# Squared-ReLU attention and a routed expert layer on one core: straight query copies for the score matmuls

## The chip, the cores and the metric

The kernel runs on one core of a Trainium2 chip. TensorE multiplies matrices into PSUM, VectorE, ScalarE and GpSimd work elementwise, and SyncE only issues DMAs. The metric is the device time of one execution in microseconds. The profile calls the engines PE (PEld for TensorE's weight loads), DVE, ACT, POOL and SP.

## The reference

There are 8 sequences of 2496 tokens with 256 channels. Attention has no softmax: the scores are the product of z (64 wide) with itself. The expert layer routes each token whose skip score is positive to one of 8 experts.

```python
scores = (1 / S) * np.matmul(z, z.transpose(0, 2, 1))
attn = np.maximum(scores, 0.0) ** 2
x = (u * np.matmul(attn, v)).reshape(B * S, D)

do_compute = x @ w_skip > 0
xc = x[do_compute]
e_idx = np.argmax(xc @ w_gate, axis=1)     # gate_w: the softmax's largest value
for e in range(E):                          # 8 experts, 256 -> 1024 -> 256
    h = np.maximum(xc[mask] @ w1[e], 0.0)
    y[mask] = gate_w[mask, None] * (h @ w2[e])
out = x.copy(); out[do_compute] = xc + y
```

## The kernel before

**Chunks and steps.** The queries of a sequence (a batch, `b`) are taken in five chunks, `c` = 0 to 4: four of 512 and one of 448. This makes 40 chunks, `ci` = 5 b + c. For each chunk the keys are walked in ten steps `p` of 256 keys; `order` gives the order of the ten, and `k` is the place in it. In the numbers of the planner one chunk is `NB` = 20, so `at(s0 + 10, f)` runs `f` at the end of the chunk's step k = 5.

**Precision.** Each float32 operand is split into a high part that TensorE takes and the rest, `zh` and `zl`, `vh` and `vl`, `ah` and `al`; a product is three matmuls (high x high, high x low, low x high).

**A step.** `scores` (L242) multiplies the z of 256 keys (stationary) with the queries of the chunk (moving) into the PSUM tile `ps` (L251): three products for two groups of 128 keys, six matmuls, which are 64 deep and so run in pairs, one in each half of the array. ScalarE makes `r` from `ps` (ReLU L292, square L293). ScalarE or VectorE rounds `r` to `ah` (L315), and VectorE subtracts to get `al` (L319). `attend` (L346) multiplies v (stationary) with `ah` and `al` (moving) into the accumulators `acc`: 24 matmuls, 12 pairs, in a step, 18 in the one with p = 9. Step s makes the scores and weights of step s + 2 (`LA`), so TensorE has the scores of a later step between the attention matmuls of the current one.

**Recalled scores.** The score matrix of a batch is symmetric. For the pairs of chunks in `PAIRS` the weights are turned by VectorE (L268), written to `kept` and read back by SyncE (`recall`, L280) in place of computing them. Steps with recalled weights have no score matmuls.

**The order of tokens.** z and v are stored on the host with each 512 tokens in an order of their own (blocks of 32, the two block indices exchanged), so that recalled blocks fit. As keys, tokens are taken as they lie. As queries they must be in token order: `queries` (L235) reads a chunk of 512 with three nested loops, 16 runs of 32 columns. Chunks of 448 are read straight.

**End of a chunk.** `finish` multiplies by u and turns the result to rows `xrow`, which SyncE writes to `xr` and `out`. `routing` finds each token's expert and place for two chunks at a time; GpSimd writes the tokens to the experts' lists by indirect DMA (`put_in`, L505: two at the end of each of four steps, in the second half of one chunk and at k = 1 of the next). In the attention part this is GpSimd's only regular work.

**Experts.** After the 40 chunks `unit` handles 256 tokens at a time: GpSimd fetches their rows by indirect DMA (L556; VectorE first copies the indices, `go`, L554), TensorE turns them and does the two layers (L605, L624), VectorE adds to `o` (L653), and GpSimd scatters it to `out` (L654). Weights of the next expert are converted meanwhile, by GpSimd from expert 2 on (L151, L157).

**Buffers and order.** v and expert weights share `VBUFS` rotating tiles of 2 KB per partition: 20 per batch, two (`vh`, `vl`) for each of ten pairs of key blocks, and 16 per expert. `o` has two buffers of 2 KB and `o3` two of 1 KB in a pool of their own. Each engine executes its instructions in program order, which is written out by hand; between engines there are semaphores only. So GpSimd may run ahead of the step in whose code its instruction stands, as far as its operands and buffers allow.

Of the kernel before, what the change touches and what calls it, by code (L numbers as in the profile page):

```python
# [8 lines left out]
F32 = mybir.dt.float32  # L9
F32R = mybir.dt.float32r  # L10
# [7 lines left out]
P = 128  # L18
QC = 512
# [23 lines left out]
def f32(ap):  # L43
    return ap.bitcast(F32)
# [3 lines left out]
def attn_moe(ctx, tc, zT, uT, v, wg, w1, w2, cst, pad, out):  # L48
# [4 lines left out]
    nc = tc.nc  # L53
    B, _, SZ = zT.shape
    S = uT.shape[3]
    D = 2 * P
# [28 lines left out]

    zt, vt = {}, {}
    wts = {}
    VBUFS = 35

    def vtile(name):  # L90
        return vp.tile([P, 2, D], F32R, name=name, tag="v", bufs=VBUFS)
# [140 lines left out]
    kept = {x: dram.tile([QC, QC], F32, name="kept%d%d" % x) for x in PAIRS}  # L232
    HALF = (slice(0, 64), slice(64, 128))

    def queries(z, h, n):  # L235


        if n < QC:
            return z[h, :n]
        return z[h].rearrange("p (b a i) -> p a b i", b=4, a=4)  # L240

    def scores(b, q0, n, p):  # L242

        ps = ps_s.tile([P, 2, QC], F32, name="ps", tag="s")
        zh, zl = zt[b, p // 2]
        qh, ql = zt[b, q0 // QC]
        for m, (k, q) in enumerate(((zh, qh), (zh, ql), (zl, qh))):
            for x, h in enumerate(HALF):
                o = (2 * p + x) % 4 * P
                to = ps[:, x, :n] if n < QC else ps[:, x].rearrange("p (a b i) -> p a b i", b=4, a=4)  # L250
                nc.tensor.matmul(to, k[h, o : o + P], queries(q, h, n), start=(m == 0), stop=(m == 2))  # L251
        return ps

    def r_tile():
# [30 lines left out]
    def weights(ci, p, r=None, at_end=False):  # L285

        b, q0, n = chunks[ci]
        old, new = r, (ci % NQ, p // 2) in pairs(b)
        if not old:
            ps = scores(b, q0, n, p)  # L290
            r = r_tile()
            nc.scalar.activation(r[:, :, :n], ps[:, :, :n], AF.Relu, scale=isc)  # L292
            nc.scalar.activation(r[:, :, :n], r[:, :, :n], AF.Square)  # L293
        views, got = [], []

        def high():
            ah = ap.tile([P, 2, QC], F32R, name="ah", tag="ah")
            al = ap.tile([P, 2, QC], F32R, name="al", tag="al")
            got.extend((ah, al))
            if old and n < QC:  # L300

                b3 = 3 * P
                for x in range(2):
                    views.append(
                        [r.rearrange("p x (a k e) -> p x k a e", a=4, k=4)[:, x, :3]]
                        + [t[:, x, :b3].rearrange("p (k a e) -> p k a e", a=4, k=3) for t in (ah, al)]
                    )
                views.append(
                    [r.rearrange("p x (a k e) -> p x k a e", a=4, k=4)[:, :, 3, : (n - b3) // 32, :]]
                    + [t[:, :, b3:n].rearrange("p x (a e) -> p x a e", e=32) for t in (ah, al)]  # L310
                )
            else:
                views.append([x[:, :, :n] for x in (r, ah, al)])
            for r_, h_, _ in views:
                (nc.scalar.copy if on_act(ci, p) else nc.vector.tensor_copy)(h_, r_)  # L315

        def low():
            for r_, h_, l_ in views:
                nc.vector.tensor_sub(l_, r_, f32(h_))  # L319
            if new:  # L320
                if at_end:
                    put_off.append(lambda: keep(ci, p, r))
                else:
                    keep(ci, p, r)

        return got, high, low
# [252 lines left out]
    def unit(e, w, ids, xg, xt, fills=()):  # L579


        W = w * P
        xh, xl = xt
        w1h, w1l, w2t = wts[e]

        yb = [ps_acc.tile([P, 2, D], F32, name="y", tag="acc") for _ in range((w + 1) // 2)]
        ys = [yb[t // 2][:, t % 2, :] for t in range(w)]
        G = 2 if w < 3 else 1
        hs = []

        def h_part(p):
            ps = ps_h.tile([P, QC], F32, name="psh", tag="h")

            hh, hl = (
                ap.tile([P, 2 * QC], F32R, name="h" + c, tag=tag, bufs=k)[:, 80 : 80 + QC]
                for c, tag, k in (("h", "r", 5), ("l", "a" + "hl"[p % 2], 3))
            )
            for j in range(G):
                f = G * p + j
                m = 0  # L600
                for d in range(2):
                    k = 2 * d + f // 4
                    a, o = divmod((f % 4) * P, D)
                    for wt, x in ((w1h[k], xh), (w1h[k], xl), (w1l[k], xh)):
                        nc.tensor.matmul(  # L605
                            ps[:, j * W : (j + 1) * W], wt[:, a, o : o + P], x[:, d, :W],
                            start=(m == 0), stop=(m == 5),
                        )
                        m += 1
            nc.scalar.activation(hh[:, : G * W], ps[:, : G * W], AF.Relu)  # L610
            nc.vector.scalar_tensor_tensor(  # L611
                hl[:, : G * W], ps[:, : G * W], 0.0, f32(hh[:, : G * W]), op0=ALU.max, op1=ALU.subtract
            )
            hs.append((hh, hl))

        def y_part(p0, p1):

            fs = range(G * p0, G * p1)
            order = [(f, t) for t in range(w) for f in fs]
            for f, t in order:  # L620
                hh, hl = hs[f // G]
                tt = slice((f % G) * W + t * P, (f % G) * W + (t + 1) * P)
                for m, (h, k) in enumerate(((hh, 0), (hh, 1), (hl, 0))):
                    nc.tensor.matmul(  # L624
                        ys[t], h[:, tt], w2t[f][:, k, :],
                        start=(f == 0 and m == 0 and t % 2 == 0), stop=(f == NF - 1 and m == 2),
                        skip_group_check=True,
                    )

        np_ = NF // G  # L630
        last = np_ - 2
        parts = [(h_part, p) for p in range(3)]
        for p in range(3, np_):
            parts += [(h_part, p), (y_part, p - 3, p - 2)]
        if np_ == 4:
            parts += [(y_part, 1, 2)]
        else:
            last = np_ - 3
        parts += [(y_part, last, np_)]
        fills = dict(fills)  # L640
        for k, (f, *p) in enumerate(parts):
            f(*p)
            for g in fills.pop(k, ()):
                g()
        for k in sorted(fills):
            for g in fills[k]:
                g()
        o = op.tile([P, 2, D], F32, name="o", tag="o")
        for t in range(w):
            if t == 2:  # L650
                o = op.tile([P, 1, D], F32, name="o3", tag="o3")
            ot = o[:, t % 2, :]
            nc.vector.scalar_tensor_tensor(ot, ys[t], f32(ids[:, t, 1:2]), xg[t], op0=ALU.mult, op1=ALU.add)  # L653
            put = nc.gpsimd.indirect_dma_start(  # L654
                out=out,
                out_offset=bass.IndirectOffsetOnAxis(ap=ids[:, t, 0:1], axis=0),
                in_=ot,
                in_offset=None,
                bounds_check=N - 1,
                oob_is_err=False,  # L660
            )
            if t:
                tc.declare_no_dep(put.ins, put0.ins, reason="the rows of a unit's tokens are distinct")
            put0 = put
# [11 lines left out]
    def at(s, f):  # L676

        todo.setdefault(s // 2, []).append(f)
# [30 lines left out]
    for ci, (b, q0, n) in enumerate(chunks):  # L709
        s0 = ci * NB  # L710
        if ci + 1 < NC:
            at(s0 + 12, lambda ci=ci: load_u(ci + 1))
        if ci == 0:
            first = [(4 * j - 8, j % 2, 3, load_z, j) for j in range(2, NZ)]
            first += [(2 * g - 4, 1, 4, load_v, g) for g in range(2, NB // 2)]
            for s1, _, k, load, j in sorted(first, key=lambda x: x[:2]):
                eng = nc.vector
                if s1 - k < 0:
                    at(s1, load(0, j, eng))
                else:  # L720
                    later(s1 - k, k, load, 0, j, eng)
            at(14, lay_pads)
        if q0 == 0 and b + 1 < B:

            jobs = [(load_v, 0, 1, 3), (load_z, 0, 1, 6), (load_v, 1, 2, 3), (load_z, 1, 2, 5), (load_v, 2, 2, 7)]
            jobs += [(load_v, 3, 3, 3), (load_v, 4, 3, 4), (load_v, 5, 3, 6), (load_v, 6, 3, 7)]
            jobs += [(load_v, 7, 4, 2), (load_z, 2, 4, 3), (load_v, 8, 4, 4), (load_z, 3, 4, 5)]
            jobs += [(load_v, 9, 4, 6), (load_z, 4, 4, 7)]
            for load, j, c, k in jobs:
                later(s0 + c * NB + 2 * k - 7, 7, load, b + 1, j, nc.vector)  # L730
# [285 lines left out]
```

## Time and profile before

| | |
|---|---|
| median of 3 runs | 1785.65 us (1785.43 to 1788.15) |
| the profiled execution | 1782.95 us, of which the span from the first to the last instruction is 1781.2 us |
| attention part | to about 1276 us of the span |
| granted TensorE clock | 0.999 |
| busy | PE 1760.8 us, DVE 1185.5, ACT 1159.5, POOL 446.9 |

A busy share is an average over the attention and the expert part. In a line of instruction groups stand the code line, engine, operation, output<-inputs, shapes, the count, the busy time, the mean of one in ns, and the idle time of the engine before them with what ended it. In the chain of waits a piece is a stretch in which the chain stayed on one line of one engine.

### The profile page before, as it was taken

Reading aid. Unit: us, or ns where it says so; the run is one execution under the profiler, and the core shown is the slowest. Engines: PE = TensorE matmul, PEld = TensorE weight load, DVE = VectorE, ACT = ScalarE, POOL = GpSimd, SP = SyncE. Lnnn points to the kernel's source line nnn. Section 1 sums busy time; section 2 is a strip of 40 time slices with the busy share of each in tenths; the row PEclk is TensorE's granted clock in tenths of the full one; section 3 lists DMA queues with packets and bytes.
Section 4 is the critical chain, followed back from the end, with each engine's and each line's share of the span. In section 5 each row is a group of like instructions: output and inputs, shape, how many; then the busy total and the mean of one; then the engine's idle time right before and its main releaser. Section 6 shows DMA issues by size and latency. Waiting matters only on the chain.

```text
span 1781.2 us, 40579 instructions
## 1 busy us (share of the span) xinstructions
PE 1760.8 (99%) x15844; PEld 1555.9 (87%) x15844; DVE 1185.5 (67%) x2113; ACT 1159.5 (65%) x1499; POOL 446.9 (25%) x421
## 2 busy tenths in 40 slices
PE   8999999999999999999999999999999999999997
PEld 6879878987887898788889888888999999999997
DVE  6877877787887787788778778777753433343332
ACT  8878877877788777778777877877633333333321
POOL 0102201211220120121112022012255556635621
PEclk9999999999999999999999999999999999999999
DMA  5476689478857947894794789488652323313210
GB/s 190 125 181 151 158 211 223 98 200 220 177 140 193 230 104 195 213 211 109 199 219 117 189 206 222 112 191 196 158 120 76 91 84 110 95 52 90 87 38 26
DMA packets 403763, 267.44 MB, mean 150 GB/s; under 512 B 205859, under 2 KB 334117, under 8 KB 403440
## 3 DMA queue, kind: packets, MB, share of 16 engines
q1 hardware_dynamic: 389440, 240.47, 55.2%
q0 software_dynamic: 13712, 22.99, 4.6%
q8 instruction: 141, 2.31, 0.6%
q14 instruction: 182, 1.49, 0.3%
q10 hardware_dynamic: 288, 0.17, 0.0%
HBM read 145.80 MB, written 118.39 MB: 148 GB/s over the span
## 4 chain that ended last, share of the span: by engine, by line
PE 86%; DMA 4%; ACT 3%; DVE 3%; issue 2%; SPq 1%; POOL 0%; DVEq 0%; POOLq 0%; ACTq 0%
PE acc L346 52%; PE psh L605 11%; PE y L624 11%; PE ps L251 10%; DMA out<-o,idt 2%; DVE al L319 2%; DMA r<-kept 1%; ACT ah L315 1%; PE psm L414 1%; SPq L280 1%; ACT r L292 1%; ACT r L293 1%; PE pst L574 1%; DVE rt L268 0%; DMA xr<-xrow 0%
## 5 line engine op out<-in xcount | busy, mean ns | idle before, releaser
L346 PE MATMUL acc<-ah,vh 64*128 64x512 f32 (+1 forms) x3120 | 661.6, 385 | 1.3 <-DVE ah L315 1.1
L346 PE MATMUL acc<-ah,vl 64*128 64x512 f32 (+1 forms) x3120 | 644.0, 383 | 0.0
L319 DVE TENSOR_TENSOR al<-r,ah 128x1024 fp32r<-128x1024 f32 (+3 forms) x464 | 479.1, 1048 | 190.9 <-ACT ah L315 181.1
L346 PE MATMUL acc<-al,vh 64*128 64x512 f32 (+1 forms) x3120 | 514.1, 385 | 1.5 <-DVE al L319 0.9
L505 POOL DMA_INDIRECT lst<-pair,dest x160 | 198.0, 1238 | 1052.1 <-DVE dest L503 952.4
L346 PEld LDWEIGHTS acc<-ah,vh 64*128 64x128 f32 x3120 | 347.2, 184 | 56.5 <-ACT ah L315 2.8
L292 ACT ACTIVATE r<-ps 128x1024 f32<-128x1024 f32 (+1 forms) x278 | 280.1, 1007 | 178.9 <-PE ps L251 170.0
L346 PEld LDWEIGHTS acc<-ah,vl 64*128 64x128 f32 x3120 | 346.0, 184 | 50.3 <-DVE vl L120 0.2
L346 PEld LDWEIGHTS acc<-al,vh 64*128 64x128 f32 x3120 | 320.8, 184 | 59.0 <-DVE al L319 10.9
L315 ACT CAST ah<-r 128x1024 fp32r<-128x1024 f32 (+3 forms) x381 | 330.4, 892 | 51.2 <-PE acc L346 38.3
L293 ACT ACTIVATE r<-r 128x1024 f32<-128x1024 f32 (+1 forms) x278 | 289.9, 1043 | 8.8
L610 ACT ACTIVATE hh<-psh 128x512 fp32r<-128x512 f32 (+1 forms) x172 | 98.8, 583 | 286.8 <-PE psh L605 246.6
L605 PE MATMUL psh<-xt,w1h 128*128 128x256 f32 (+1 forms) x1280 | 235.1, 285 | 2.3 <-issue 1.8
L624 PE MATMUL y<-w2t,hh 128*128 128x256 f32 x1328 | 235.9, 281 | 0.0
L611 DVE SCALAR_TENSOR_TENSOR hl<-psh,hh 128x512 fp32r<-128x512 f32 (+1 forms) x172 | 113.0, 670 | 137.2 <-ACT hh L610 129.3
L624 PEld LDWEIGHTS y<-w2t,hh 128*128 128x128 f32 x1328 | 202.3, 189 | 0.6 <-issue 0.6
L605 PEld LDWEIGHTS psh<-xt,w1h 128*128 128x128 f32 x1280 | 197.4, 189 | 3.2 <-issue 3.2
L624 PE MATMUL y<-w2t,hl 128*128 128x256 f32 x664 | 184.7, 278 | 1.3 <-DVE hl L611 1.3
L605 PE MATMUL psh<-xt,w1l 128*128 128x256 f32 (+1 forms) x640 | 181.9, 284 | 0.0
L268 DVE STREAM_TRANSPOSE rt<-r 128x512 f32<-128x512 f32 x244 | 158.3, 686 | 1.6 <-DMA kept<-rt 1.5
L251 PE MATMUL ps<-zh 64*128 64x512 f32 (+1 forms) x556 | 126.0, 398 | 4.8 <-ACT zh L108 4.8
L624 PEld LDWEIGHTS y<-w2t,hl 128*128 128x128 f32 x664 | 124.7, 188 | 1.6 <-DVE hl L611 1.5
(170 smaller groups left out, 1610.3 us busy)
## 6 DMA issues: line engine op xcount, KB each, us to landing
kept<-rt SPq DMA_DIRECT2D x244, 256.0 KB
r<-kept SPq DMA_DIRECT2D x488, 128.0 KB
raw<-in_v SPq DMA_DIRECT2D x80, 256.0 KB
ut<-in_uT SPq DMA_DIRECT2D x32, 512.0 KB
xr<-xrow SPq DMA_DIRECT2D x128, 128.0 KB
out<-xrow SPq DMA_DIRECT2D x128, 128.0 KB
raw<-in_w SPq DMA_DIRECT2D x64, 256.0 KB
zf<-in_zT SPq DMA_DIRECT2D x40, 256.0 KB
```

Source lines behind the costliest of these rows:

```text
L251: nc.tensor.matmul(to, k[h, o : o + P], queries(q, h, n), start=(m == 0), stop=(m == 2))
L268: nc.vector.transpose(t[:, :, 32 * k : 32 * k + 32], r[:, x, :].rearrange("p (m i) -> p m i", i=32))
L292: nc.scalar.activation(r[:, :, :n], ps[:, :, :n], AF.Relu, scale=isc)
L293: nc.scalar.activation(r[:, :, :n], r[:, :, :n], AF.Square)
L315: (nc.scalar.copy if on_act(ci, p) else nc.vector.tensor_copy)(h_, r_)
L319: nc.vector.tensor_sub(l_, r_, f32(h_))
L346: nc.tensor.matmul(acc[t][:, :n], w[h, x, dd], a[h, x, :n], start=(first and t not in halves[:m]), stop=(last and t not in halves[m + 1 :]),)
L505: put = nc.gpsimd.indirect_dma_start(out=lst, out_offset=bass.IndirectOffsetOnAxis(ap=dest[:, t : t + 1], axis=0), in_=pair[:, t, :], in_o ...
L605: nc.tensor.matmul(ps[:, j * W : (j + 1) * W], wt[:, a, o : o + P], x[:, d, :W], start=(m == 0), stop=(m == 5),)
L610: nc.scalar.activation(hh[:, : G * W], ps[:, : G * W], AF.Relu)
L611: nc.vector.scalar_tensor_tensor(hl[:, : G * W], ps[:, : G * W], 0.0, f32(hh[:, : G * W]), op0=ALU.max, op1=ALU.subtract)
L624: nc.tensor.matmul(ys[t], h[:, tt], w2t[f][:, k, :], start=(f == 0 and m == 0 and t % 2 == 0), stop=(f == NF - 1 and m == 2), skip_group_c ...
```

## The change

For every chunk of 512 queries but the very first, GpSimd copies the z tiles of the queries (`zh` and `zl`) once into tiles `zq` in token order (`straight`); the copy stands in the code at the end of step k = 5 of the chunk before. The score matmuls of these chunks then read a flat row of 512 columns and write a flat row of PSUM. The copies need four tiles of 2 KB per partition. They come from `o` and `o3`, whose tiles now rotate in the same buffers, and from one tile less for v and weights.

```diff
-    VBUFS = 35
+    VBUFS = 34
...
-    def queries(z, h, n):
-        if n < QC:
-            return z[h, :n]
-        return z[h].rearrange("p (b a i) -> p a b i", b=4, a=4)
-
-    def scores(b, q0, n, p):
+    zq = {}
+
+    def straight(ci):
+        b, c = ci // NQ, ci % NQ
+        zq[ci] = [zp.tile([P, QC], F32R, name="zq" + x, tag="zq" + x, bufs=2) for x in "hl"]
+        for t, z in zip(zq[ci], zt[b, c]):
+            nc.gpsimd.tensor_copy(
+                t.rearrange("p (a b i) -> p a b i", a=4, b=4),
+                f32(z).rearrange("p (b a i) -> p a b i", b=4, a=4),
+            )
+
+    def queries(ci, k, h, n):
+        if n < QC or ci in zq:
+            return (zq[ci] if ci in zq else zt[ci // NQ, ci % NQ])[k][h, :n]
+        return zt[ci // NQ, ci % NQ][k][h].rearrange("p (b a i) -> p a b i", b=4, a=4)
+
+    def scores(ci, p):
+        b, _, n = chunks[ci]
         ps = ps_s.tile([P, 2, QC], F32, name="ps", tag="s")
         zh, zl = zt[b, p // 2]
-        qh, ql = zt[b, q0 // QC]
-        for m, (k, q) in enumerate(((zh, qh), (zh, ql), (zl, qh))):
+        flat = n < QC or ci in zq
+        for m, (k, q) in enumerate(((zh, 0), (zh, 1), (zl, 0))):
             for x, h in enumerate(HALF):
                 o = (2 * p + x) % 4 * P
-                to = ps[:, x, :n] if n < QC else ps[:, x].rearrange("p (a b i) -> p a b i", b=4, a=4)
-                nc.tensor.matmul(to, k[h, o : o + P], queries(q, h, n), start=(m == 0), stop=(m == 2))
+                to = ps[:, x, :n] if flat else ps[:, x].rearrange("p (a b i) -> p a b i", b=4, a=4)
+                nc.tensor.matmul(to, k[h, o : o + P], queries(ci, q, h, n), start=(m == 0), stop=(m == 2))
...
-            ps = scores(b, q0, n, p)
+            ps = scores(ci, p)
...
-        o = op.tile([P, 2, D], F32, name="o", tag="o")
+        o = zp.tile([P, 2, D], F32, name="o", tag="zqh", bufs=2)
...
-                o = op.tile([P, 1, D], F32, name="o3", tag="o3")
+                o = zp.tile([P, 1, D], F32, name="o3", tag="zql", bufs=2)
...
+            if chunks[ci + 1][2] == QC:
+                at(s0 + 10, lambda ci=ci: straight(ci + 1))
```

## The prediction

> **What bounds the kernel now.** I read the page first: which engine is busy, at what clock, and who carries the chain that ended last.
>
> ```profile
> PE 1760.8 (99%) x15844; PEld 1555.9 (87%) x15844; DVE 1185.5 (67%) x2113; ACT 1159.5 (65%) x1499; POOL 446.9 (25%) x421
> ...
> PEclk9999999999999999999999999999999999999999
> ...
> PE 86%; DMA 4%; ACT 3%; DVE 3%; issue 2%; SPq 1%; POOL 0%; DVEq 0%; POOLq 0%; ACTq 0%
> ```
>
> TensorE is busy for 99% of the span, at full granted clock throughout, and holds 86% of the chain. So time is won by making its instructions shorter, and lost by anything that makes it wait. The question is therefore how long a score matmul with the broken-up queries takes beside one with a straight operand. Means of single matmuls don't tell this, because two matmuls run in the two halves of the array at once and overlap their neighbours. The chain of waits does: where it stays on TensorE, a piece's length is the pace of its matmuls. Its columns are start us, length us, and what.
>
> ```profile
> 375.15 0.70 PE ps L251 x6
> 375.85 2.76 PE acc L346 x24
> 378.61 0.70 PE ps L251 x6
> 379.31 2.76 PE acc L346 x24
> ...
> 392.60 0.70 PE ps L251 x6
> 393.30 6.16 PE acc L346 x54
> 399.46 0.70 PE ps L251 x6
> 400.16 6.84 PE acc L346 x60
> 407.00 0.70 PE ps L251 x6
> ```
>
> All of these are 512 columns wide. Read three things. First, six score matmuls, three pairs, take 0.70 us: 0.233 a pair. Second, the attention matmuls have two paces. The piece of 60 is longer than the piece of 24 by 36 matmuls, or 18 pairs, and by 6.84 - 2.76 = 4.08 us: 0.2267 a pair. The piece of 54 gives the same, (6.16 - 2.76) / 15 = 0.2267. But the first 12 pairs behind a score group take 2.76 us, 0.230 each. So TensorE needs some pairs after a score group to fall back into its even pace, and these cost 2.76 - 12 x 0.2267 = 0.04 us. Third, a whole step with scores takes 0.70 + 2.76 = 3.46 us, where 15 even pairs would take 3.40. A score group thus costs 0.02 us itself and 0.04 us behind itself.
>
> Is it the broken-up operand, or scores as such? The last chunk of a batch has 448 columns, and its queries are read straight already:
>
> ```profile
> 301.81 0.61 PE ps L251 x6
> 302.42 1.22 PE acc L346 x12
> 303.63 0.61 PE ps L251 x6
> 304.24 3.65 PE acc L346 x36
> ```
>
> Scores: 0.61 / 3 = 0.203 a pair. Attention right behind them: 1.22 / 6 = 0.203, and over 18 pairs 3.65 / 18 = 0.203. There is neither a dearer score pair nor a slow stretch behind it. So I put both down to the operand in 16 runs of 32 columns.
>
> **The change part by part.**
>
> *Straight queries.* How many groups change:
>
> ```profile
> L251 PE MATMUL ps<-zh 64*128 64x512 f32 x460 | 106.7, 405 | 4.8 <-ACT zh L108 4.8
> L251 PE MATMUL ps<-zl,zh 64*128 64x512 f32 x460 | 104.5, 395 | 0.0
> L251 PE MATMUL ps<-zh,zl 64*128 64x512 f32 x460 | 104.3, 394 | 0.0
> ```
>
> 3 x 460 = 1380 matmuls are 230 groups of six. The first chunk of batch 0 has ten steps and no copy, so 220 groups change: 220 x (0.02 + 0.04) = 13.2 us of TensorE time. Bounds: nothing, if flat scores stay at 0.233 a pair, and 13.2 if they take the even pace and don't break it. I take 13.2, because attention matmuls switch weights, moving tile and output bank inside those long pieces without losing the pace, and a straight score matmul differs from them in nothing else.
>
> *How much of it reaches the end.* The attention part's chain (20 to 1276 us):
>
> ```profile
> by line: PE acc L346 72.0%; PE ps L251 13.9%; DVE al L319 2.0%; DMA r<-kept 1.9%; ACT ah L315 1.6%; SPq L280 1.5%; PE psm L414 1.5%; ACT r L292 1.3%; ACT r L293 1.3%; issue 0.8%; DVE rt L268 0.6%; DMA xr<-xrow 0.4%; DVE pre L462 0.2%; SPq L
> ```
>
> TensorE holds 72.0 + 13.9 + 1.5 = 87% of it. Elsewhere (weights al and ah just in time at the turn of a chunk, recalled scores) a faster TensorE only waits longer; late next there is al. So 0.87 x 13.2 = 11.5 us.
>
> *The copies.* Two per chunk for 31 chunks: 62 more GpSimd instructions of 128x512, one operand in, one out. No such row exists; the nearest are these.
>
> ```profile
> L151 POOL TENSOR_TENSOR w1l<-raw,w1h 128x512 fp32r<-128x512 f32 x24 | 30.9, 1298 | 0.5
> L187 POOL CAST tri<-cs 128x128 bf16<-128x128 f32 x1 | 0.3, 289 | 2.9 <-DMA cs<-in_cst 2.9
> L194 POOL MEMSET run_cnt<- 128x8 bf16 x1 | 0.1, 98 | 0.0
> ```
>
> From 98 ns at 8 columns and 289 at 128 come 1.6 ns a column and an estimate of 0.29 + 384 x 0.0016 = 0.9 us. The ends are 0.65 (half the two-operand one) and 1.3. So 1.8 us a chunk on an engine that is mostly idle. When they run is set by GpSimd's own queue, which in the attention part holds only the list writes:
>
> ```profile
> 327.23 1.16 POOL L505 DMA_INDIRECT lst<-pair,dest  x1 [2.00 <-DVE dest L503]
> ...
> 340.79 0.97 POOL L505 DMA_INDIRECT lst<-pair,dest  x1 [3.75 <-DVE dest L503]
> 342.07 1.83 POOL L505 DMA_INDIRECT lst<-pair,dest  x1 [0.30 <-issue]
> 390.98 1.71 POOL L505 DMA_INDIRECT lst<-pair,dest  x1 [47.08 <-DVE dest L503]
> ```
>
> A copy is queued after the writes of the second step of its chunk at the latest, or of the chunk before, and waits only for z tiles loaded long ago and for the scores of the straight chunk two before it. So it is done three steps to a chunk ahead of its first score matmul, and TensorE's new wait for it costs nothing; were that cover gone, it would cost up to 31 x 1.8 = 56 us. Behind the copies stand the next list writes, 47 us idle in front; 1.8 us there harms nobody. No DMA is added, and SyncE's queue keeps its order.
>
> *What the copies do to VectorE.* Here the trace shows a price, in the expert part:
>
> ```profile
> L554 DVE COPY go<-idt x45: 151/159/2031, 1308.1 to 1729.4; 128x2 int32<-128x2 int32 x45
> ```
>
> A two-column copy that takes 159 ns at the median took up to 2031 while GpSimd worked on weights: VectorE can be held for as long as GpSimd's elementwise work. Whether al (two inputs in SBUF) is held too, no row shows: no such VectorE instruction meets GpSimd elementwise work. What a held al costs depends on whether TensorE is waiting for it:
>
> ```profile
> L319 DVE TENSOR_TENSOR al<-r,ah x464: 276/1218/1284, 10.0 to 1279.3; 128x1024 fp32r<-128x1024 f32 x107, 128x384 fp32r<-128x384 f32 x24, 128x896 fp32r<-128x896 f32 x16, 128x128 fp32r<-128x128 f32 x8
> ...
>   PEld acc L346: 10.9, 24
> ...
>   PE acc L346: 0.9, 5
> ```
>
> TensorE waited for al at 29 of 400 steps (7%); elsewhere al is early. If a pair of copies meets two al, half of the time with GpSimd first, each held 0.9 us, the loss is 31 x 2 x 0.07 x 0.9 / 2 = 2.0 us. Bounds: 0 (never held) and 31 x 1.8 = 56 us (every hold reaches TensorE in full); I take 2.0, near the lower end, for the 7%.
>
> *One v buffer fewer.* 34 buffers are 17 pairs. Pair 7, 8 or 9 of the next batch now takes what pair 0, 1 or 2 of this one held. They are converted after steps 2, 4 and 6 of the batch's last chunk, and pairs 0, 1 and 2 are read last in steps 1, 1 and 2. The last weights of expert 0 take pair 0 of the last batch, five steps after its last read. So nothing waits; with the cover gone, ScalarE would wait for up to one step, 3.4 us, at each batch. *Result tiles in the copies' buffers:* the same two deep, and first written when scores are long over: nothing. *Straight score output:* the old view was already in order in memory: nothing.
>
> **Sum.** -11.5 + 2.0 = -9.5 us against this execution's 1782.95 us (span 1781.2): 1773.4. The runs' median, 1785.65, lies 2.7 above it, and I forecast that: 1776.1.
>
> **The rivals.** *Only the score pairs gain* (the stretch behind them stays slow, being due to the switch of work): 0.87 x 220 x 0.02 = 3.8 us less 2.0, 1783.8. For it: some slowness also follows other work. Against it: the 448-column pieces.
>
> *The runs of 32 cost nothing.* The 0.233 would then be the scores' own, the gain 0, and the time 1785.65 + 2.0 = 1787.7. Against it speaks 0.203 beside 0.203 above; for it, that 448 columns never show the even pace (0.2267 x 448 / 512 would be 0.198), so that the two widths may not compare. By the Trainium skill ("SBUF — State Buffer", section "Specifications (TRN2)") reads lose only where a 16-byte line gets fewer than two hits; a run of 32 words fills eight lines, so by that page this rival holds. The 0.70 us against 0.68 for three even pairs speaks against that page, unless the runs cost elsewhere than in the lines.
>
> *Slower: copies hold VectorE at the turn of a chunk.* If each chunk's copies hold an al that TensorE is waiting for by one copy, the price is 31 x 0.9 = 28 us, less 11.5: 1802. It decides from 11.5 / 31 = 0.37 us per chunk on. For it speaks the 2031 ns; against it the 7%, and that half of the copies start behind the second step's list writes, away from the turn. The Trainium skill ("SBUF — State Buffer", section "SBUF: two separate sides") says that VectorE and GpSimd share a port pair as an exclusive lock, which a VectorE instruction with two SBUF inputs needs as well; the row of go agrees for a plain copy, and no run here shows it for al.
>
> **How the numbers follow.** Both gains 0.52, 1773 to 1780; only score pairs 0.20, 1782 to 1786; nothing gained 0.15, 1785 to 1789; slower by holds 0.13, 1790 to 1803. From 1772 (13.2 gained, no loss) to 1788 some 0.85 are inside; the likeliest case alone has 1773 to 1780. A measurement of this kernel tells 0.2%, 3.6 us, from no change. Faster: 0.52 and a little of the second case, 0.54. Slower: 0.13. Same: 0.33.
>
> **What would show it.** In the chain, score groups of 0.68 us instead of 0.70 and 24 attention matmuls behind them in 2.72 instead of 2.76; if the second stays at 2.76, the first rival holds, if both stay, the second. A GpSimd group of 62 copies near 0.9 us. An al group whose longest is far over 1284 ns and a larger wait of TensorE for al would show the holds. The prediction is wrong if straight scores break the even pace too, or if the saved time comes back as waits for al.

## The result and the profile after

The changed kernel takes 1773.57 us (median of 4 runs, 1771.19 to 1776.28) beside 1786.9 us for the kernel before: a ratio of 0.9934, 95% interval 0.9922 to 0.9946, or 11.8 us less (9.6 to 13.9). This is the recorded ratio; the quotient of the two medians is 0.9925, or 13.3 us. Two more sets of runs gave 0.9932 (0.9918 to 0.9945) and 0.9944 (0.9930 to 0.9957). It is faster by more than the runs scatter, and lies inside the predicted 1772 to 1788; the forecast was 1776.1.

The group of al from the page of the kernel before, then TensorE's busy line and the group of al from the page of the changed kernel:

```profile
L319 DVE TENSOR_TENSOR al<-r,ah 128x1024 fp32r<-128x1024 f32 (+3 forms) x464 | 479.1, 1048 | 190.9 <-ACT ah L315 181.1
```

```profile
PE 1751.5 (99%) x15844; PEld 1571.7 (89%) x15844; DVE 1196.0 (67%) x2113; ACT 1159.2 (65%) x1499; POOL 491.4 (28%) x483
...
L331 DVE TENSOR_TENSOR al<-r,ah 128x1024 fp32r<-128x1024 f32 (+3 forms) x464 | 488.4, 1068 | 185.2 <-ACT ah L327 175.4
```

TensorE has the same 15844 matmuls in 9.3 us less busy time. VectorE has the same 2113 instructions and is busy for 10.5 us more: al rose from 479.1 to 488.4 us in total.

In that first profile the chain breaks off at the end of the kernel; in a second execution of the same kernel (label change_again below) it is whole. The same stretch as in the prediction:

```profile
377.48 0.68 PE ps L263 x6
378.16 2.72 PE acc L358 x24
380.88 0.68 PE ps L263 x6
...
391.27 0.68 PE ps L263 x6
391.95 6.12 PE acc L358 x54
398.07 0.68 PE ps L263 x6
398.75 6.80 PE acc L358 x60
```

A score group takes 0.68 us where it took 0.70, and the 24 attention matmuls behind it 2.72 where they took 2.76. Long pieces have shrunk by the same 0.04 only (6.80 from 6.84): it was their first pairs that were slow. 2.72 / 12 = 0.2267 us: straight scores keep the even pace, and a scored step takes 3.40 us in place of 3.46.

The copies, from line L242 of the same second execution (duration min/median/max in ns):

```profile
L242 POOL CAST zqh<-zh x31: 622/642/1413, 6.6 to 1177.2; 128x512 fp32r<-128x512 f32 x31
L242 POOL CAST zql<-zl x31: 605/626/1644, 7.7 to 1178.5; 128x512 fp32r<-128x512 f32 x31
```

### The profile page after: what moved, and what is told of

Read it like the earlier page. It is cut to its first block, busy times and chain, and to the rows that moved or that the text cites. A ratio compares the mean times of both kernels' runs of the same rounds, so it can differ in the third digit from the quotient of the medians.

```text
span 1772.5 us, 40706 instructions
## 1 busy us (share of the span) xinstructions
PE 1751.5 (99%) x15844; PEld 1571.7 (89%) x15844; DVE 1196.0 (67%) x2113; ACT 1159.2 (65%) x1499; POOL 491.4 (28%) x483
## 5 line engine op out<-in xcount | busy, mean ns | idle before, releaser
L358 PE MATMUL acc<-ah,vh 64*128 64x512 f32 (+1 forms) x3120 | 654.6, 383 | 1.2 <-DVE ah L327 0.6
L331 DVE TENSOR_TENSOR al<-r,ah 128x1024 fp32r<-128x1024 f32 (+3 forms) x464 | 488.4, 1068 | 185.2 <-ACT ah L327 175.4
L358 PE MATMUL acc<-al,vh 64*128 64x512 f32 (+1 forms) x3120 | 506.3, 383 | 2.2 <-DVE al L331 1.6
L666 POOL DMA_INDIRECT out<-o,idt x77 | 76.7, 996 | 171.4 <-DVE o L665 148.6
```

The source lines that it names most:

```text
L358: nc.tensor.matmul(acc[t][:, :n], w[h, x, dd], a[h, x, :n], start=(first and t not in halves[:m]), stop=(last and t not in halves[m + 1 :]),)
L666: put = nc.gpsimd.indirect_dma_start(out=out, out_offset=bass.IndirectOffsetOnAxis(ap=ids[:, t, 0:1], axis=0), in_=ot, in_offset=None, bou ...
```

## The experiments

**How they are compared.** Some kernels read the queries in another token order; then other tokens go to other experts, and the expert part has other work (15768 matmuls in place of 15844 with straight scores and no copies, 15694 and 15666 with runs of 8 and of 128). The first chunk also differs between executions of one kernel (34.0 to 34.5 us in the traces that have TensorE at full clock from 8 or 9 us of the span on, 35.5 to 36.5 where that comes at 13 to 14 us). So besides the ratios of whole runs I use a stretch that all have in common: in the chain, the long attention piece of batch 0's last chunk (x132) and that of the very last chunk (x96) each stand at the same place of the program in every kernel. From the start of one to the start of the other are 35 chunks: batches 1 to 7, with 10 + 8 + 6 + 4 = 28 scored steps of 512 columns each, 196 groups. In order: the changed kernel; the kernel before in a second execution; straight scores without copies; copies alone.

```profile
146.90 13.38 PE acc L358 x132
...
1255.45 10.12 PE acc L358 x96
```

```profile
147.71 13.38 PE acc L346 x132
...
1263.94 10.12 PE acc L346 x96
```

```profile
146.39 13.38 PE acc L346 x132
...
1254.84 10.12 PE acc L346 x96
```

```profile
147.31 13.38 PE acc L358 x132
...
1263.65 10.12 PE acc L358 x96
```

| label | median us | ratio to before, 95% | stretch us |
|---|---|---|---|
| before_again | 1783.18 | 1.0004 (0.9995 to 1.0013) | 1116.23 |
| change_again | 1771.2 | 0.9932 (0.9918 to 0.9945) | 1108.55 |
| change_third | 1772.31 | 0.9944 (0.9930 to 0.9957) | |
| flat_no_copies | 1768.27 | 0.9912 (0.9899 to 0.9926) | 1108.45 |
| copies_alone | 1783.33 | 0.9999 (0.9990 to 1.0008) | 1116.34 |
| buffers_alone | 1784.98 | 1.0002 (0.9993 to 1.0011) | |
| copies_on_scalar_engine | 1781.72 | 0.9989 (0.9980 to 0.9998) | 1114.36 |
| copies_three_times | 1794.98 | 1.0066 (1.0050 to 1.0081) | |
| one_product_in_runs | 1780.63 | 0.9984 (0.9975 to 0.9994) | 1114.07 |
| runs_of_8 | 1785.24 | 1.0009 (1.0000 to 1.0018) | 1127.46 |
| runs_of_128 | 1757.89 | 0.9856 (0.9841 to 0.9871) | |

Where the stretch is empty, the chain broke off, as in the first profile. The prediction's execution of the kernel before has 1262.64 - 146.30 = 1116.34: the stretch repeats within about 0.1 us. The change is worth 7.7 us in it.

**The mark: the changed kernel again (change_again).**

> The changed kernel, run again beside the three below. Every theory: 0.9934 of the kernel before, about 12 us less. It serves as the mark for the other runs of the same chip.

As expected.

**Straight scores without copies (flat_no_copies).**

```diff
-        return z[h].rearrange("p (b a i) -> p a b i", b=4, a=4)
+        return z[h]
...
-                to = ps[:, x, :n] if n < QC else ps[:, x].rearrange("p (a b i) -> p a b i", b=4, a=4)
+                to = ps[:, x, :n]
```

> The kernel before, but the score matmuls read the z tile of the queries as it lies in memory, one run of 512 columns. There are no copies, and buffers are as before. What is left out: the queries are not brought into token order, so the outputs belong to the wrong tokens; the number and size of all instructions are those of the kernel before. My theory (the runs of 32 columns cost TensorE 0.02 us per score group and 0.04 us behind it, and the copies cost a little): all 230 groups gain, 230 x 0.06 x 0.87 = 12 us, and the copies' price of about 2 us is not paid, so this is 1 to 3 us faster than the changed kernel, near 1773. Rival A (the copies cost nothing): the same time as the changed kernel within 1 us. Rival B (the gain of the change comes from something else, the new buffers or the copies' effect on other engines): no gain over the kernel before.

The whole run is 2.9 us shorter than the changed kernel's, which looks like the price of the copies that my theory foretold. It isn't: the stretch is 1108.45 against 1108.55, and the rest is the expert part with its 76 matmuls less (483.7 us from the last attention matmul to the last matmul, beside 487.3). So the straight operand alone gives the gain (rival B falls), and the copies cost nothing where they can be compared (rival A).

**Copies that nobody reads (copies_alone).** Only the test in `queries` and `flat` is taken back:

```diff
-        flat = n < QC or ci in zq
+        flat = n < QC
```

> The changed kernel with all its copies and buffers, but the score matmuls read the z tiles in 16 runs of 32 as before; nobody reads the copies. My theory: the gain is gone and the copies' holds of VectorE remain, 0.5 to 4 us slower than the kernel before (1787 to 1791); the longest al near 2400 ns as in the changed kernel, TensorE's wait for al up by 1 to 2 us. Rival A (the copies cost nothing): within 0.5 us of the kernel before. Rival B (the gain came from buffers or copies): about 12 us faster than before.

1116.34 in the stretch, 0.9999 in the runs: no gain and no loss. My 0.5 to 4 us of loss is refuted, although VectorE is held just as in the changed kernel, as the line of al shows (kernel before, second execution, then copies alone):

```profile
L319 DVE TENSOR_TENSOR al<-r,ah x464: 278/1218/1228, 10.0 to 1280.6; 128x1024 fp32r<-128x1024 f32 x107, 128x384 fp32r<-128x384 f32 x24, 128x896 fp32r<-128x896 f32 x16, 128x128 fp32r<-128x128 f32 x8
```

```profile
L331 DVE TENSOR_TENSOR al<-r,ah x464: 278/1220/2401, 9.8 to 1280.3; 128x1024 fp32r<-128x1024 f32 x107, 128x384 fp32r<-128x384 f32 x24, 128x896 fp32r<-128x896 f32 x16, 128x128 fp32r<-128x128 f32 x8
...
  PEld acc L358: 10.5, 23
...
  PE acc L358: 1.0, 5
```

The longest al doubles, and TensorE's wait for al (10.5 and 1.0 us) is what it was in the kernel before (10.5 and 1.0).

**What a hold looks like (changed kernel, timeline: start us, us, instruction).**

```profile
469.67 0.64 POOL L242 CAST zqh<-zh 128x512 fp32r<-128x512 f32 x1
470.00 2.39 DVE L331 TENSOR_TENSOR al<-r,ah 128x384 fp32r<-128x384 f32 x1
470.23 0.63 POOL L242 CAST zql<-zl 128x512 fp32r<-128x512 f32 x1
470.79 0.63 POOL L242 CAST zqh<-zh 128x512 fp32r<-128x512 f32 x1
```

Two chunks' copies stand together here, four in a row to about 471.97. The al that starts within the first takes 2.39 us where its like takes 0.54 (the mean of that shape in the kernel before), and gets its turn only when the last has ended. The same happens at four places of the execution, each in the last chunk of a batch, where al is early enough. It isn't so everywhere. At three other places an al gets in between the two copies of a pair:

```profile
596.65 1.70 DVE L331 TENSOR_TENSOR al<-r,ah 128x1024 fp32r<-128x1024 f32 x1 [2.73 <-ACT ah L327]
```

```profile
596.62 0.65 POOL L242 CAST zqh<-zh 128x512 fp32r<-128x512 f32 x1
597.18 1.64 POOL L242 CAST zql<-zl 128x512 fp32r<-128x512 f32 x1
```

This al ends 1.09 us after the first copy, and the second copy takes 1.64 us, to 598.82, in place of some 0.63. What decides whether VectorE gets in between two copies is not shown.

**Three times the copies (copies_three_times).**

```diff
-        for t, z in zip(zq[ci], zt[b, c]):
+        for t, z in 3 * list(zip(zq[ci], zt[b, c])):
```

> The changed kernel with each copy made three times, one after the other: 186 copies, up to 3.8 us of GpSimd in a row. Theory 1 (VectorE has room for being held, al is mostly early, which is why the 62 copies cost nothing): al grows by another 10 to 25 us in total, its longest to 3 us or more, but the chunks 1 to 39 of the attention part grow by less than 3 us over the changed kernel's 1230.8. Theory 2 (one pair of copies just fits, more doesn't): 5 us or more slower than the changed kernel. Beside that: TensorE's pause of about 2 us at the branch into the last expert, which the profiled kernels show except for the changed one; if it depends on where the code lies, it may come back here.

Theory 1 has failed: 1795 us against 1772, and al grew by 34.8 us where it allowed 10 to 25. The timeline at the same place, with twelve copies in a row, and TensorE's waits for al over the whole run:

```profile
476.31 0.65 POOL L242 CAST zqh<-zh 128x512 fp32r<-128x512 f32 x1
476.64 6.83 DVE L331 TENSOR_TENSOR al<-r,ah 128x384 fp32r<-128x384 f32 x1
```

```profile
  PEld acc L358: 26.9, 29
...
  PE acc L358: 15.6, 10
```

The al is held for 6.83 us, and here it is too late: TensorE waits 3.48 us for it, and right afterwards its granted clock is halved for 3.41 us (0.83 on average from 484 to 494 us; the score group at 486.35 takes 1.12 us). The wait and half of the 3.41 us, an estimate of what the clock costs, make 5.2 of the 5.3 us that such a chunk loses. The loss sits only where two chunks' copies meet, every second batch: these last chunks take 32.9 to 34.0 us where they take 27.6, four times some 5.3 us or more (6.4 in the first, where the clock is halved for 6.83 us), while six copies in a row (some 3.4 us) cost nothing: apart from the first, the other chunks are within 0.1 us of the changed kernel's. So theory 2 holds at four places, and theory 1 everywhere else. The changed kernel's four copies in a row still fit; there is no wide margin.

**Copies on ScalarE (copies_on_scalar_engine).**

```diff
-            nc.gpsimd.tensor_copy(
+            nc.scalar.copy(
```

> The changed kernel with the 62 copies on ScalarE in place of GpSimd. If the holds of VectorE by GpSimd are what keeps part of the gain back, the longest al falls back to about 1284 ns, and this is up to 2 us faster than the changed kernel, unless ScalarE's own 62 x 0.6 = 37 us, put in the order of its queue, make r and ah late. If the holds cost nothing, it is the same or slower: ScalarE is busy for 79% of the attention part, and two copies of 0.6 us in front of the next r cost up to 31 x 1.2 = 37 us where TensorE is waiting. I expect between 1 us faster and 4 us slower than the changed kernel.

The longest al is back at 1229 ns, and yet 1114.36 in the stretch: three quarters of the gain are lost (5.8 of 7.7 us), more than I allowed for; in whole runs it is 10.5 us slower than the changed kernel's 1771.2, where I expected 4 at most. TensorE's weight loads now wait for al 36 times:

```profile
  PEld acc L358: 15.8, 36
```

The holds were harmless; ScalarE's own work in their place is not. TensorE's waits for ah grew too, from 5.5 to 11.1 us (matmuls and weight loads together), so I read it as ah coming late and al behind it; no run tries this alone.

**Where the score pairs' time comes from: the number of runs (runs_of_128, runs_of_8).** Other factors in `queries`, no copies:

```diff
-        return z[h].rearrange("p (b a i) -> p a b i", b=4, a=4)
+        return z[h].rearrange("p (b a i) -> p a b i", b=2, a=2)   # or b=8, a=8
...    # and the same factors in the view `to` of the output in `scores`
```

> The kernel before, without copies, but the score matmuls of the chunks of 512 read the queries in 4 runs of 128 columns in place of 16 of 32. What is left out: the token order of the queries, so the outputs belong to the wrong tokens (and the routing in the expert part differs); all instructions are of the same number and size. Theory 1 (a broken-up operand costs TensorE per run: 6.5 ns a pair for 16 runs, so 0.4 ns per run): a score pair takes 0.2267 + 0.0016 = 0.228 us. Theory 2 (any pattern of more than one loop costs a fixed 6.5 ns): 0.233 as before. Behind the score group: whether an excess as small as that breaks the even pace of 0.2267 is open; if it does, the next nine pairs take 0.231 as before, if not, 0.227.

> The kernel before, without copies, but the queries are read in 64 runs of 8 columns. What is left out: the token order of the queries, as in the run with 4 runs. Theory 1 (a cost per run): 0.2267 + 64 x 0.0004 = 0.253 us a score pair, 3 x 0.020 us more per score group than before, so some 230 x 0.06 = 14 us slower than the kernel before, less what waits hide. Theory 2 (a fixed cost for the pattern): 0.233, the time of before. Theory 3 (only runs shorter than a line of SBUF cost, which 8 words of 4 bytes are not): 0.233 at most.

Four runs, timeline of TensorE (its chain broke off), and 64 runs, chain:

```profile
375.37 0.39 PE L251 MATMUL ps<-zh 64*128 64x512 f32 x2
375.60 0.39 PE L251 MATMUL ps<-zl,zh 64*128 64x512 f32 x2
375.82 0.39 PE L251 MATMUL ps<-zh,zl 64*128 64x512 f32 x2
...
378.77 0.39 PE L251 MATMUL ps<-zh 64*128 64x512 f32 x2
```

```profile
380.85 0.77 PE ps L251 x6
381.63 2.76 PE acc L346 x24
384.39 0.77 PE ps L251 x6
```

With four runs a scored step takes 378.77 - 375.37 = 3.40 us: nothing is left of the excess, of the pair or behind it. With 64 a pair takes 0.77 / 3 = 0.257 us (0.253 expected), and behind it stands the same 2.76 as with 16. So the cost goes by the number of runs, some 0.4 to 0.5 ns each, not by the pattern having several loops (theory 2), and a run of 8 words costs as well as one of 32 (theory 3). The 2 ns that four runs should cost by this don't show. With 16 and with 64 runs the pace is lost, with 4 it isn't. The kernel with 64 runs is 11.2 us longer in the stretch than the kernel before, where 196 groups at the expected 0.06 us make 11.8 (the 14 was for 230). That its runs come out at 1.0009 is due to the other routing, as is most of the 0.9856 with four runs: from the last attention matmul to the last matmul they take 479.4 and 472.0 us, the kernel before 489.4. In all these runs the output view changes together with the queries. It lies in order in memory every time, so I put the cost down to the queries; no run changes one without the other.

**The slow pairs behind a group (one_product_in_runs).** The first product in 16 runs, the other two straight:

```diff
+                flat = n < QC or m != 0
...    # where flat, the matmul reads q[h, :n] and writes ps[:, x, :n]
```

> The kernel before, without copies: of the three products of a score group only the first reads its queries in 16 runs of 32, the other two read one run of 512. What is left out: the token order of the queries in two products. Theory 1 (one slow pair is enough to break the even pace, which comes back some nine pairs later): the first pair takes 0.233, and the following pairs 0.230 on average over about ten, so a scored step keeps most of its excess, 3.44 to 3.46 us. Theory 2 (the excess behind the group grows with the number of slow pairs): a third of the excess, 3.42 us per scored step.

```profile
380.98 0.69 PE ps L252 x6
381.68 2.75 PE acc L347 x24
384.43 0.07 PE psm L482 x4
```

384.43 - 380.98 = 3.45 us, as theory 1 has it; a third of the excess would have been 3.42. One slow pair is enough: the pace is lost by being broken, not by how much. In the stretch only 2.2 of the 7.7 us are gained.

**Buffers alone (buffers_alone).** `VBUFS = 34`, and `o` and `o3` in the pool of the z tiles:

> The kernel before with the buffers of the changed kernel only: 34 tiles for v and weights, and the result tiles o and o3 in the pool of the z tiles; no copies, score matmuls as before. My theory: no wait is added, the kernel before within 0.1% (0.999 to 1.001). Rival (the places of the tiles matter in the expert part, which would explain why the attention part of the two profiled executions shrank by only 9 us and the runs by 12): 1 to 3 us faster than before, with a shorter expert part.

1.0002 (0.9993 to 1.0011): no effect, as the count of last reads said. The rival falls.

**Second and third executions (before_again, change_third).**

> The kernel before, unaltered, for a second profiled execution and as a mark of what a ratio near 1 is worth. Every theory: 0.999 to 1.001; chunks 1 to 39 of the attention part 1239.6 us as in the first; the first chunk anywhere from 34 to 36.5 us, since its loads differ from execution to execution; TensorE's pause of about 2 us at the branch into the last expert is there again if it belongs to this code.

> The changed kernel, unaltered, for a third profiled execution. Open is why the runs gained 12 us and the chunks 1 to 39 only 8.8. Theory 1 (the pause at the branch into the last expert is gone in the changed kernel, by where its code lies): no pause over 1 us at that branch here either, and the expert part 2 us shorter than in the kernel before. Theory 2 (the pause comes and goes by chance): it appears here, and the 3 us stay unexplained.

The kernel before against itself gives 1.0004, so the ratios can be trusted to about 0.1%. The pause at the branch into the last expert (some 450 us into the expert part) is there again, 1.5 us in the row of TensorE's waits that end in "issue" (the branch itself took part):

```profile
PE psh L605 <- issue: 1.5, 1, 1.5
```

With copies alone it is 2.2 us, and it is in the profiles of buffers alone, straight scores without copies, ScalarE's copies and one product too. It is in none of the three profiles of the changed kernel, nor with three times the copies. So it is hardly chance, but what it hangs on is not shown: no one part of the change takes it away. Nor is the expert part clearly 2 us shorter without it: from the last attention matmul to the last matmul the two executions of the kernel before take 489.4 and 487.7 us, the three of the changed kernel 490.0, 487.3 and 486.5.

## Why the prediction was right, point by point

**Two costs of the runs, in the score pairs and behind them: right, in size too.** 0.68 and 2.72 us stand where they were forecast. The first rival (only the score pairs gain) falls with 2.72; the second (the runs cost nothing), with the line rule of the Trainium skill ("SBUF — State Buffer", section "Specifications (TRN2)") beside it, falls with the runs of 8: those fill two 16-byte lines with four hits each, and cost the most. The row also gives a penalty for each cross to a new line, but 512 words lie in 128 lines in every one of these orders.

**How much reaches the end: the step that was too high.** I took 87%, TensorE's share of the chain. In the stretch it is 7.7 of 196 x 0.06 = 11.8 us, 65%. A share of the chain says where time lies, not what work stands behind each score group. Three things were left out. First, other work breaks the pace too. In the changed kernel, the gate matmuls (L426) and the list positions (L493):

```profile
370.13 1.00 PE psm L426 x26
371.13 2.94 PE acc L358 x24
...
384.28 0.07 PE psm L493 x4
384.35 0.78 PE ps L263 x6
385.13 2.75 PE acc L358 x24
```

And the gates in the kernel before, second execution:

```profile
372.68 1.00 PE psm L414 x26
373.68 2.94 PE acc L346 x24
```

And the list positions in its first execution, from the same stretch as the prediction's chain:

```profile
385.53 0.07 PE psm L481 x4
385.60 0.79 PE ps L251 x6
386.39 2.75 PE acc L346 x24
```

Behind the gates 2.94 us before and after; behind the list positions 0.78 + 2.75 in place of 0.79 + 2.75. Next to nothing is gained there. Second, TensorE waits longer for al (changed kernel):

```profile
  PEld acc L358: 11.1, 23
...
  PE acc L358: 1.7, 6
```

That is 1.3 us more than the 10.5 and 1.0 of the kernel before. The copies aren't the cause: straight scores without copies have 11.3 and 1.7, so the longer wait goes with the faster TensorE. Third, each batch's first score groups are made in the last chunk of the batch before, and behind them stand attention matmuls of 448 columns, which gain nothing: 21 of them take 2.23 us before and after. The prediction had seen that they have no slow stretch, and counted these groups in full.

The second executions of both kernels show how much each costs, if one takes the time from every score group to the next and compares group by group. Of the 4.1 us that are missing, 1.2 are missing behind the list positions (14 groups), 0.8 at or behind the gates (28), 1.0 before the 448-column matmuls (17), and 0.7 at seven other groups with a wait of TensorE in them. The other 130 groups gain 0.058 us each, nearly the 0.06 of the forecast, and account for most of the last 0.4.

**The copies' price: 0 in place of 2.0 us.** They ran where I put them, behind the list writes or when the scores of an earlier chunk were done, at 0.63 us (median) rather than 0.9. That they can hold al was right, and is now shown (the row of go was weaker evidence than I took it for: its 2.03 us span an indirect DMA of GpSimd as well as a weight instruction of 1.30). By the Trainium skill ("SBUF — State Buffer", section "SBUF: two separate sides") a two-input VectorE instruction needs the pair of ports that GpSimd's reading locks, and the 2.39 us agree. That page has the lock for one instruction; here it lasted for four, and elsewhere for one. It works the other way as well: a copy that meets a running al takes some 1.41 us, and one before which al got in up to 1644 ns. The step that failed is the 7% of tight al, spread evenly over the kernel. The 29 waits are 24 steps, five of them counted twice, and they have their places: in the kernel before, 16 lie in the first tenth of a chunk and 8 at 0.63 to 0.67 of one, while nearly all copies of the changed kernel run at 0.33 to 0.38 or at 0.75. The slower rival has its mechanism, but not its place; with three times the copies a held al comes too late at four places, at 5 to 6 us each, in the last chunk of a batch and not at the turn.

**The wait for the copies and the buffers: nothing, as said.** Copies alone and buffers alone lie within 0.1% of the kernel before.

**The sum.** 220 groups at 0.06 us and 65% give 8.6 us, and the copies 0: this is what the chunks 1 to 39 gained in the traces (1239.6 to 1230.8). The three sets of runs gained 11.8, 12.1 and 10.0. The pause at the branch, 1.5 to 2.2 us that I hadn't foreseen, could bring 8.6 to between 10 and 11, but that it reaches the end isn't shown, and 1 to 3 us of the gain stay open. The forecast of 9.5 is near partly by luck: a share that was too high met a price that was too high and a gain that wasn't known.

## What to carry to other kernels

Measure the pace of a matmul stream from long and short pieces of the chain: a difference of 0.007 us a pair between two kinds of matmul was hidden in means of single instructions, and two thirds of what it cost lay in the work behind it. A copy that straightens an operand which is read many times is worth it on an idle engine, if it runs where the engines that share its ports have room; give it to an engine that is early, and not too much of it in a row. An engine's share of the chain (87% here) need not be the share of a gain on it that reaches the end (65%); look at what follows each piece that gets shorter.

## What the runs showed of the hardware

Matmuls that run in pairs and read 512 columns have an even pace of 0.2267 us a pair. A single pair whose operand comes in 16 runs breaks it, and the next nine or ten pairs take some 0.04 us more in all; behind gates and list positions the pace is broken too. Attention matmuls of 448 columns behind a score group took as long with runs as without (2.23 us for 21). A moving operand in 16 runs costs 6 ns a pair, in 64 some 30, in 4 nothing that shows. GpSimd copies in a row can keep VectorE's two-input instruction out until the last has ended (2.39 us behind four, 6.83 behind twelve, where 0.54 is usual), but at other places it got in after the first. After TensorE had waited 3.48 us, its granted clock was halved for 3.41 us.
